# Relu squared in place, one sum per block on GpSimd from block 4 on, and a new order

## The chip, the cores and the metric

The kernel runs on one core of a Trainium2 chip. The metric is the time of one execution in microseconds (us) of device time. Five engines take part, each with its own instruction queue worked off in order: PE (TensorE, matmuls and weight loads), DVE (VectorE), ACT (ScalarE), POOL (GpSimd) and SP (SyncE, which only issues DMAs here). POOL issues DMAs too.

## The reference

Eight batches of eight heads of sparse attention (half of the heads with a local mask of 32, half with a strided one), followed by a feed-forward layer with a squared relu:

```python
B, H, S, D = 8, 8, 576, 64
scores = np.where(masks, q @ k.T / sqrt(D), -1e9)
attn = softmax(scores)
x = (attn @ v).transpose(0, 2, 1, 3).reshape(4608, 512)
h = x @ w_in                      # 512 -> 2048
r = np.maximum(h, 0.0)
out = (s * (r * r) + b) @ w_out   # 2048 -> 512, s and b are single numbers
```

## The kernel before

All matmuls are in 16-bit floats. The 4608 tokens are cut into nine blocks T = 0 to 8 of 512 tokens. The attention of the eight batches (b = 0 to 7, two pairs of local heads and two of strided heads each) makes the rows of x, which the blocks consume. For a block, the first product (`ff1`) makes h in 16 tiles of 128 rows by 512 tokens in PSUM, relu brings each tile to SBUF, and a square of two tiles at a time makes g, the tile `gT` with 16 x 512 columns. There are two `gT` buffers. Relu writes a small buffer `u` (pool `up`, three of 128 x 2 x 512), and the square reads `u` twice and writes `gT`:

```python
nc.scalar.activation(out=u, in_=gts["h", T, ft], func=AF.Relu)
nc.vector.tensor_tensor(out=g, in0=u, in1=u, op=ALU.mult)   # or Square on ACT
```

The second product is done for blocks 2 to 8 by a scheme with seven products P1 to P7 instead of eight (`ff2_seven`). It needs four sums of quarters of `gT`, made in two halves h = 0, 1 of 128 x 1024 elements each (`sums_post`): S3 (a difference, into a tile `S` of its own, of which there is one), then S1, S2 and S4, which all build on S3. S3 of block T can be made only when P7 of block T-1 has read the tile `S`. P7 reads S3, P5 reads S1, P6 reads S2, P3 reads S4. Between the products DVE evicts partial results (`Va`, `Ua`, `Vb`, and `o`, which goes to DRAM), and several products wait for such an eviction before they add to the same PSUM bank: P3 waits for the `o` made from P5 and `Vb`. `Ub` is `Ua` plus a row of constants.

For blocks 7 and 8 the first product is done by a seven-product scheme too (`ff1_seven`), with sums of the weights and of x made on DVE (lines 1099 and 1116), and with additions on DVE in place of some of the relus (line 1161).

Attention steps that matter below: the exponentials come from ACT into `p_loc` or `p_str`, DVE multiplies these by the mask (line 682), then PE multiplies them with v (line 717), and DVE divides by the row sums (lines 734 and 744).

The order of every queue is fixed when the program is made. A planner (`Plan`) walks through a model of the engines: PE steps are taken in an order set by due times, and other work is posted with its needs and its cost on each engine that could do it, and taken in the order of the time at which it became ready plus an offset from a table (`ORDER`, four tables for four stretches of the plan, about 55 numbers each). Nothing is reordered at run time: an engine whose next instruction waits makes everything behind it wait.

POOL issues the loads of q, k and v (`fetch_qk`, `fetch_v`). Ahead of the loads of a batch stand two tiny copies to `gate` (line 1356), which make the queue wait until the transposes of an earlier batch have read their source.

Of the kernel before, what the change touches and what calls it, by code (L numbers as in the profile page):

```python
# [139 lines left out]
class Step:  # L140
    def __init__(self, fn, ns, needs=(), group=None, keys=(), posts=(), after=None):
# [5 lines left out]
ORDER = [  # L147
# [39 lines left out]
]  # L187
# [34 lines left out]
def lay_out(ctx, tc, nc, q, k, v, moe_w_in, moe_w_out, moe_s, moe_b, out, order, q_shape, out_shape,  # L222
# [7 lines left out]
    PS = 512  # L230
# [32 lines left out]
    recp = ctx.enter_context(tc.tile_pool(name="recp", bufs=4))  # L263
    up = ctx.enter_context(tc.tile_pool(name="up", bufs=3))
    gp = ctx.enter_context(tc.tile_pool(name="gp", bufs=2))
# [553 lines left out]
    FIRST7 = NBLK - 2  # L819
    SUM_P = None  # L820
    H = NFT // 2

# [13 lines left out]
    def sums_post(T):  # L836

        at2, at4 = ("S2", "S4") if roomy(T) else ((0, 0), (0, 1))
        for h in range(2):
# [18 lines left out]
            free = [("P7", T - 1)] if T > SEVEN else []  # L858
            plan.post(gl + free, ns, make("S", (0, 0), (1, 0), ALU.subtract), [("S", T, 3, h)])
            plan.post(gh + [("S", T, 3, h)], ns, make((1, 0), (1, 0), (1, 1), ALU.add),  # L860
# [145 lines left out]
    def ff1(T, ft, ct, group, cts=(0, 1, 2, 3), early=False):  # L1006
# [23 lines left out]
        if ct == cts[-1]:  # L1030
            key = ("h", T, ft)
            s.keys = [key] + ([("F1", T)] if ft == NFT - 1 else [])

            at = ff_order(T).index(ft)
            pair = tuple(ff_order(T)[at // 2 * 2:at // 2 * 2 + 2])

            def rl(eng):
                if at % 2 == 0:
                    gts["u", T, pair] = up.tile([128, 2, PS], FP16, tag="u", name="u")
                u = gts["u", T, pair][:, at % 2]  # L1040
                if eng == "A":
                    nc.scalar.activation(out=u, in_=gts["h", T, ft], func=AF.Relu)  # L1042
                else:
                    nc.vector.tensor_relu(out=u, in_=gts["h", T, ft])

            def sq(eng):
                u = gts["u", T, pair]
                g = gts[T][:, pair[0]:pair[0] + 2, :]
                if eng == "A":
                    nc.scalar.activation(out=g, in_=u, func=AF.Square)  # L1050
                else:
                    nc.vector.tensor_tensor(out=g, in0=u, in1=u, op=ALU.mult)  # L1052

            first = at // 2 * 2
            free = ([("g", T, ff_order(T)[first - 6])] if first >= 6 else
                    [("g", T - 1, ff_order(T - 1)[first - 6])] if T else [])
            s.posts = [([key] + free, {"A": 600, **({"V": 690} if T == 0 else {})}, rl, [("u", T, ft), group])]
            if at % 2:
                s.posts.append(([("u", T, x) for x in pair],
                                {"V": 700, **({"A": 1055} if T >= SQ_ACT else {})}, sq,  # L1060
                                [("g", T, x) for x in pair]))
# [58 lines left out]
    def ff1_seven():  # L1120
# [3 lines left out]
        for at, (T, u) in enumerate(units):  # L1124
# [27 lines left out]

            def u_at(row, j, st=st, ft=ft):
                if ("u", row) not in st:
                    st["u", row] = (xnp if row else up).tile(
                        [128, 2, PS], FP16, tag="xs" if row else "u", name="u")
                return st["u", row][:, :, 256 * j:256 * j + 256]

# [15 lines left out]

            def square(row, st=st, T=T, ft=ft):
                def g(eng):
                    if T not in gts:
                        gts[T] = gp.tile([128, NFT, PS], FP16, tag="gT", name="gT")
                    x = st["u", row]
                    g_ = gts[T][:, ft + 8 * row:ft + 8 * row + 2, :]  # L1180
                    if eng == "A":
                        nc.scalar.activation(out=g_, in_=x, func=AF.Square)
                    else:
                        nc.vector.tensor_tensor(out=g_, in0=x, in1=x, op=ALU.mult)
                return g

            def key(x, id_=id_):
                return (x,) + id_

            def was(x, old=old):  # L1190
                return [(x,) + old] if old else []

            far = ff_order(T - 1)[8 + 4 * u:12 + 4 * u] if u < 2 else [
                x + y for x in (ft - 4, ft + 4) for y in (0, 1)]
            free = [("g", T - 1 if u < 2 else T, x) for x in far]
            COPY = {"A": 600.0, "V": 690.0}
# [11 lines left out]
            def wn(n, ft=ft):  # L1208
# [17 lines left out]
                         [key("c21"), Dd]),  # L1226
                        ([key("c21"), key("c22"), ("F2", T - 2)], SQR, square(1),
                         [("g", T, ft + 8), ("g", T, ft + 9)])]),
                "P3": ("A", A, False, s_of(4), x_of(1, 1), xn(1, 1), wn(4) + [key("fe")],
                       [([key("p3")] + free, COPY, relu, [key("c12"), A]),  # L1230
                        ([key("c11"), key("c12"), ("F2", T - 2)], SQR, square(0),
                         [("g", T, ft), ("g", T, ft + 1)])]),
# [405 lines left out]
```

## Time and profile before

| what | value |
|---|---|
| runs | 297.03, 297.75 and 298.77 us, median 297.75 |
| profiled execution, first to last instruction | 295.5 us (the page gives no other time of it) |
| PE busy | 289.5 us, 98% |
| DVE busy | 236.8 us, 80%, 498 instructions |
| ACT busy | 194.6 us, 66%, 334 instructions |
| POOL busy | 92.8 us, 31%, 140 instructions |
| granted TensorE clock | 1.000 |

The table is from the page of the one profiled execution. An instruction counts as busy while it runs or is pipelined; a busy DVE or ACT can still have been waiting for a resource inside an instruction. Times in the views are in us from the start of the span.

### The profile page before, as it was taken

The numbers are of one execution on the slowest core, as the hardware profiler recorded it, in microseconds if no ns is written. First come the engines' busy times: TensorE is split into PE (matmuls) and PEld (weight loads), VectorE is DVE, ScalarE is ACT, GpSimd is POOL, SyncE is SP. The second block draws the span as 40 slices with busy tenths as digits, with TensorE's granted clock in tenths as the row PEclk, the third lists the DMA queues.
The fourth block names the chain that finished last, engine by engine and source line by source line (L and its number), as shares of the span: only waits on it lengthen the run. The fifth ranks groups of instructions, "written<-read, shape, count | busy, mean of one in ns | idle before, by whom it ended". The sixth has DMA issues, their size and how long they took to land.

```text
span 295.5 us, 7106 instructions
## 1 busy us (share of the span) xinstructions
PE 289.5 (98%) x2803; PEld 219.3 (74%) x2803; DVE 236.8 (80%) x498; ACT 194.6 (66%) x334; POOL 92.8 (31%) x140
## 2 busy tenths in 40 slices
PE   7899999999999999999999999999999999999995
PEld 3775655665565567989867785779888999999984
DVE  5765977888976789768986888688899689888874
ACT  3667855897967797947873777478966564576500
POOL 8872623610961396008820195200002000000000
PEclk9999999999999999999999999999999999999999
DMA  8999999999999699979999999998430300210314
GB/s 131 180 206 203 213 184 174 208 189 128 140 160 145 98 91 161 160 138 146 162 149 147 169 168 130 134 137 213 44 104 13 109 35 2 71 38 0 109 39 143
DMA packets 106152, 38.19 MB, mean 129 GB/s; under 512 B 85414, under 2 KB 103974, under 8 KB 106118
## 3 DMA queue, kind: packets, MB, share of 16 engines
q0 software_dynamic: 60848, 18.23, 64.2%
q1 hardware_dynamic: 45270, 19.51, 36.1%
q8 instruction: 22, 0.36, 0.5%
q14 instruction: 12, 0.10, 0.1%
HBM read 36.99 MB, written 10.62 MB: 161 GB/s over the span
## 4 chain that ended last, share of the span: by engine, by line
PE 95%; POOL 3%; DVE 1%; issue 1%; ACT 0%; POOLq 0%
PE ps_f L1016 32%; PE ps_f L984 25%; PE ps_f L1271 8%; PE ps_s L656 5%; PE ps_f L1241 3%; PE ps_a L717 3%; PE ps_t L1241 2%; PE ps_s L984 2%; PE ps_a L1241 2%; PE ps_s L1241 2%; PE ps_t L717 1%; PE ps_t L984 1%; PE ps_s L1271 1%; PE ps_f L717 1%; PE ps_t L535 1%; PE ps_f L535 1%
## 5 line engine op out<-in xcount | busy, mean ns | idle before, releaser
L1016 PE MATMUL ps_f<-xT,w_in_sb 128*128 128x512 f16 (+4 forms) x568 | 115.3, 331 | 0.0
L1042 ACT ACTIVATE u<-ps_f 128x512 f16<-128x512 f32 x107 | 62.8, 595 | 34.5 <-PE ps_f L1016 32.4
L1016 PEld LDWEIGHTS <-w_in_sb 128*128 128x128 f16 x576 | 57.1, 114 | 23.1
L984 PEld LDWEIGHTS <-gT 128*128 128x128 f16 x608 | 58.3, 98 | 8.6
L984 PE MATMUL ps_f<-w_out_sb,gT 128*128 128x256 f16 x376 | 53.4, 273 | 0.0
L1271 PE MATMUL ps_f<-w_out_sb,gT 128*128 128x512 f16 x112 | 31.9, 379 | 0.0
L674 ACT ACTIVATE p_str<-ps_s 72x432 f16<-72x432 f32 (+1 forms) x45 | 21.1, 488 | 10.1 <-PE ps_s L656 9.5
L1052 DVE TENSOR_TENSOR gT<-u 128x1024 f16<-128x1024 f16 x32 | 21.8, 682 | 5.2 <-ACT u L1042 4.8
L1050 ACT ACTIVATE gT<-u 128x1024 f16<-128x1024 f16 x24 | 25.4, 1058 | 0.7
L984 PE MATMUL ps_f<-w_mix,gT 128*128 128x256 f16 x176 | 24.9, 273 | 0.0
L674 ACT ACTIVATE p_loc<-ps_s 128x384 f16<-128x384 f32 x46 | 20.7, 489 | 5.5 <-PE ps_s L656 5.1
L744 DVE TENSOR_TENSOR x_nat<-ps_a,rec 72x384 f16<-72x384 f32 (+2 forms) x45 | 23.5, 523 | 0.7
L852 DVE TENSOR_TENSOR gT<-gT 128x1024 f16<-128x1024 f16 x34 | 22.4, 683 | 0.3 <-ACT gT L1050 0.3
L415 POOL DMA_DIRECT2D v_loc<-in_v_dram x24 | 17.8, 767 | 10.1 <-DMA w_out_sb<-in_moe_w_out_dram 4.2
L984 PEld LDWEIGHTS <-S 128*128 128x128 f16 x176 | 17.1, 98 | 2.7
L717 PEld LDWEIGHTS <-p_str 72*128 72x128 f16 x256 | 13.6, 98 | 5.8 <-ACT p_str L674 0.7
L420 POOL DMA_DIRECT2D v_str<-in_v_dram x16 | 13.0, 817 | 12.8 <-PE ps_f L1016 3.7
L1271 PEld LDWEIGHTS <-gT 128*128 128x128 f16 x128 | 11.4, 98 | 6.9 <-issue 0.2
L1356 POOL COPY gate<-kT 1x1 f16<-1x1 f16 x6 | 2.2, 371 | 45.0 <-DMA kT<-ks 45.0
L984 PE MATMUL ps_f<-w_mix,S 128*128 128x256 f16 x112 | 15.0, 273 | 0.0
L734 DVE RECIPROCAL rec<-ps_a 72x6 f32<-72x6 f32 (+2 forms) x45 | 8.3, 184 | 8.4 <-PE ps_a L717 8.0
L717 PEld LDWEIGHTS <-p_loc 128*128 128x128 f16 x192 | 11.2, 98 | 5.0 <-ACT kTs L437 0.8
(235 smaller groups left out, 543.1 us busy)
## 6 DMA issues: line engine op xcount, KB each, us to landing
out_dram<-o SPq DMA_DIRECT2D x34, 256.0 KB
w_in_sb<-in_moe_w_in_dram POOLq DMA_DIRECT2D x4, 512.0 KB, 9.9
w_out_sb<-in_moe_w_out_dram POOLq DMA_DIRECT2D x4, 512.0 KB, 10.7
qs<-in_q_dram POOLq DMA_DIRECT2D x6, 288.0 KB, 8.1
ks<-in_k_dram POOLq DMA_DIRECT2D x6, 288.0 KB, 9.9
v_loc<-in_v_dram POOLq DMA_DIRECT2D x24, 72.0 KB, 9.8
ql<-in_q_dram POOLq DMA_DIRECT2D x4, 288.0 KB, 9.9
kl<-in_k_dram POOLq DMA_DIRECT2D x16, 72.0 KB, 3.7
```

The source lines that it names most:

```text
L415: nc.gpsimd.dma_start(out=vl[LPAD:128, h, :, 0:D], in_=v_band(b, h))
L674: nc.scalar.activation(out=st["pw", g][0:nk, 0:2 * n * nq], in_=st["s", g][0:nk, 0:2 * n * nq], func=AF.Exp, scale=scale)
L717: nc.tensor.matmul(out=st["pa", g][:, n % 6, :], lhsT=st["pw", gp_][0:nk, i * nq:i * nq + WIDE], rhs=vt[0:nk, 2 * mm + e, j, :])
L744: nc.vector.tensor_tensor(out=x_at(0, cnt), in0=st["pa", g][0:nq, 0:cnt, 0:D], in1=st["rec", g][0:nq, 0:cnt].to_broadcast([nq, cnt, D]), o ...
L852: {"V": nc.vector, "P": nc.gpsimd}[eng].tensor_tensor(out=at(out), in0=at(x), in1=at(y), op=op)
L984: nc.tensor.matmul(out=gts[name, T, t][:, 0] if halves else gts[name, T][:, t], lhsT=lhs(k, t), rhs=rhs(k), start=fresh and k == 0 and (ha ...
L1016: nc.tensor.matmul(out=gts["h", T, ft][:, lo:hi], lhsT=w_in_sb[ft // 4][:, ct].rearrange("p (x l) -> p l x", l=4)[:, ft % 4], rhs=xT[ct][: ...
L1042: nc.scalar.activation(out=u, in_=gts["h", T, ft], func=AF.Relu)
L1050: nc.scalar.activation(out=g, in_=u, func=AF.Square)
L1052: nc.vector.tensor_tensor(out=g, in0=u, in1=u, op=ALU.mult)
L1241: nc.tensor.matmul(out=st[bk][:, 256 * t:256 * t + 256], lhsT=lhs(t, c), rhs=rhs(c), start=fresh and t == c == 0, stop=t == c == 1, skip_g ...
L1271: nc.tensor.matmul(out=gts[id_], lhsT=gts[T][:, ft, ts * 128:(ts + 1) * 128], rhs=w_out_sb[:, ft, cols], start=(ft == 0), stop=(ft == NFT ...
```

## The change

Three things are changed. Relu writes straight into `gT` and the square is done there in place, on the same elements; the buffers `u` go, and with them the waits for a free one. S3 of blocks 4 to 8 is made by POOL and not by DVE, with a planned cost of 3500 ns a half. And the four tables of offsets are new, so that the planner puts much of the work in another order.

```diff
-    up = ctx.enter_context(tc.tile_pool(name="up", bufs=3))
...
+    POOL_SUM = 4
...
             free = [("P7", T - 1)] if T > SEVEN else []
-            plan.post(gl + free, ns, make("S", (0, 0), (1, 0), ALU.subtract), [("S", T, 3, h)])
+            plan.post(gl + free, {"P": 3500.0} if T >= POOL_SUM else ns,
+                      make("S", (0, 0), (1, 0), ALU.subtract), [("S", T, 3, h)])
...
             def rl(eng):
-                if at % 2 == 0:
-                    gts["u", T, pair] = up.tile([128, 2, PS], FP16, tag="u", name="u")
-                u = gts["u", T, pair][:, at % 2]
+                u = gts[T][:, ft]
...
             def sq(eng):
-                u = gts["u", T, pair]
                 g = gts[T][:, pair[0]:pair[0] + 2, :]
                 if eng == "A":
-                    nc.scalar.activation(out=g, in_=u, func=AF.Square)
+                    nc.scalar.activation(out=g, in_=g, func=AF.Square)
                 else:
-                    nc.vector.tensor_tensor(out=g, in0=u, in1=u, op=ALU.mult)
+                    nc.vector.tensor_tensor(out=g, in0=g, in1=g, op=ALU.mult)
...
-            s.posts = [([key] + free, {"A": 600, **({"V": 690} if T == 0 else {})}, rl, [("u", T, ft), group])]
+            s.posts = [([key], {"A": 600, **({"V": 690} if T == 0 else {})}, rl, [("u", T, ft), group])]
...
-            free = [("g", T - 1 if u < 2 else T, x) for x in far]
+            free = [("F2", T - 2)]
...
 ORDER = [
-    {"g": 0.0, "S": -2500.0, "in": 500.0, "w_mix": 2500.0, "wc": 0.0, "ev": 2500.0, "c21": -200.0,
+    {"g": -400.0, "S": -200.0, "in": 500.0, "w_mix": 1500.0, "wc": 0.0, "ev": -400.0,
...
```

PE gets the same instructions as before, matmul for matmul, and the first 528 of its 2801 matmuls stand in the same order. Of the squares, 27 now stand on ACT where 36 stood, and 45 on DVE where 36 stood. One `Ub` goes from POOL to DVE.

On POOL, before, near the end of its queue, where the loads for batch 7 stand (`gate` is the copy that waits for a transpose):

```order
70 L1356 COPY gate<-kT_2571 1x1 x2
71 L387 DMA ql<-in_q_dram 96x6x64 x4
72 L387 DMA kl<-in_k_dram 96x6x64 x4
73 L405 DMA qs<-in_q_dram 72x4x512
74 L405 DMA ks_120<-in_k_dram 72x4x512
75 L415 DMA v_loc_102<-in_v_dram 96x6x64 x4
76 L420 DMA v_str_104<-in_v_dram 72x8x64 x4
77 L926 ISA
78 L926 TENSOR_TENSOR Ub<-Ua,bcs 128x512
```

And the same place of the same queue now:

```order
70 L853 ISA
71 L853 TENSOR_TENSOR S<-gT 128x1024 x2
72 L1346 COPY gate<-kT_2527 1x1 x2
73 L387 DMA ql<-in_q_dram 96x6x64 x4
74 L387 DMA kl<-in_k_dram 96x6x64 x4
75 L405 DMA qs<-in_q_dram 72x4x512
76 L405 DMA ks_117<-in_k_dram 72x4x512
77 L415 DMA v_loc_99<-in_v_dram 96x6x64 x4
78 L420 DMA v_str_101<-in_v_dram 72x8x64 x4
79 L853 TENSOR_TENSOR S<-gT 128x1024 x8
```

The two halves of S3 of block 4 stand ahead of the loads for batch 7, and the eight of blocks 5 to 8 behind them; the `Ub` is gone.

On DVE, before, where S3 of block 4 is made, from the `Vb` of block 3 on (`o` from `Vb` is the eviction that P3 waits for; the mask is that of batch 6):

```order
267 L903 SCALAR_TENSOR_TENSOR Vb<-ps_f_162,sb_all,Ub 128x512
268 L852 TENSOR_TENSOR S<-gT 128x1024 x2
269 L852 TENSOR_TENSOR gT<-gT 128x4x256
270 L915 SCALAR_TENSOR_TENSOR o<-ps_f_163,sb_all,Vb 128x512
271 L852 TENSOR_TENSOR gT<-gT 128x4x256
272 L682 TENSOR_TENSOR p_loc_115<-p_loc_115,masks 128x1152
```

The same place on DVE now:

```order
266 L905 SCALAR_TENSOR_TENSOR Vb<-ps_f_159,sb_all,Ub 128x512
267 L1051 TENSOR_TENSOR gT<-gT 128x1024
268 L917 SCALAR_TENSOR_TENSOR o<-ps_f_160,sb_all,Vb 128x512
269 L853 TENSOR_TENSOR gT<-gT 128x4x256
270 L682 TENSOR_TENSOR p_loc_112<-p_loc_112,masks 128x1152
```

The two halves of S3 are gone, a square (line 1051) stands there, and of the two halves of S1 (line 853, `gT<-gT`) only the first is still ahead of the mask.

On DVE, before, one block later, from the `Vb` of block 4 to the mask of batch 7:

```order
310 L903 SCALAR_TENSOR_TENSOR Vb<-ps_f_162,sb_all,Ub 128x512
311 L437 COPY qD_loc_108<-qTl 64x6x96 x2
312 L852 TENSOR_TENSOR S<-gT 128x1024 x2
313 L852 TENSOR_TENSOR gT<-gT 128x4x256
314 L915 SCALAR_TENSOR_TENSOR o<-ps_f_163,sb_all,Vb 128x512
315 L437 COPY v_loc_102<-v_loc_102 32x2x5x64
316 L852 TENSOR_TENSOR gT<-gT 128x4x256
317 L915 SCALAR_TENSOR_TENSOR o<-ps_f_162,sb_all,Ua 128x512
318 L682 TENSOR_TENSOR p_loc_115<-p_loc_115,masks 128x1152
```

And now:

```order
309 L905 SCALAR_TENSOR_TENSOR Vb<-ps_f_159,sb_all,Ub 128x512
310 L437 COPY qD_loc_105<-qTl 64x6x96 x2
311 L1051 TENSOR_TENSOR gT<-gT 128x1024
312 L917 SCALAR_TENSOR_TENSOR o<-ps_f_160,sb_all,Vb 128x512
313 L437 COPY v_loc_99<-v_loc_99 32x2x5x64
314 L853 TENSOR_TENSOR gT<-gT 128x4x256
315 L917 SCALAR_TENSOR_TENSOR o<-ps_f_159,sb_all,Ua 128x512
316 L682 TENSOR_TENSOR p_loc_112<-p_loc_112,masks 128x1152
```

Here too a square stands where the two halves of S3 stood, and the second half of S1 has gone behind the mask.

More of the change, by code (lines that the diff above doesn't have):

```diff
@@ L1046, in sq @@
             def sq(eng):
-                u = gts["u", T, pair]
                 g = gts[T][:, pair[0]:pair[0] + 2, :]
                 if eng == "A":
-                    nc.scalar.activation(out=g, in_=u, func=AF.Square)
+                    nc.scalar.activation(out=g, in_=g, func=AF.Square)
                 else:
-                    nc.vector.tensor_tensor(out=g, in0=u, in1=u, op=ALU.mult)
-            first = at // 2 * 2
-            free = ([("g", T, ff_order(T)[first - 6])] if first >= 6 else
-                    [("g", T - 1, ff_order(T - 1)[first - 6])] if T else [])
-            s.posts = [([key] + free, {"A": 600, **({"V": 690} if T == 0 else {})}, rl, [("u", T, ft), group])]
+                    nc.vector.tensor_tensor(out=g, in0=g, in1=g, op=ALU.mult)
+            s.posts = [([key], {"A": 600, **({"V": 690} if T == 0 else {})}, rl, [("u", T, ft), group])]
             if at % 2:
@@ L1151, in keep, with u_at @@
                 return g
[L1153 to L1157, printed above, removed]
+            def u_at(row, j, T=T, ft=ft):
+                if T not in gts:
+                    gts[T] = gp.tile([128, NFT, PS], FP16, tag="gT", name="gT")
+                return gts[T][:, ft + 8 * row:ft + 8 * row + 2, 256 * j:256 * j + 256]
             def add(row, j, of, name, st=st, u_at=u_at):
@@ L1173, in relu, with square @@
                         "p (t x) -> p t x", t=2))
-            def square(row, st=st, T=T, ft=ft):
+            def square(row, T=T, ft=ft):
                 def g(eng):
-                    if T not in gts:
-                        gts[T] = gp.tile([128, NFT, PS], FP16, tag="gT", name="gT")
-                    x = st["u", row]
                     g_ = gts[T][:, ft + 8 * row:ft + 8 * row + 2, :]
                     if eng == "A":
-                        nc.scalar.activation(out=g_, in_=x, func=AF.Square)
+                        nc.scalar.activation(out=g_, in_=g_, func=AF.Square)
                     else:
-                        nc.vector.tensor_tensor(out=g_, in0=x, in1=x, op=ALU.mult)
+                        nc.vector.tensor_tensor(out=g_, in0=g_, in1=g_, op=ALU.mult)
                 return g
@@ L1191, in was @@
                 return [(x,) + old] if old else []
-            far = ff_order(T - 1)[8 + 4 * u:12 + 4 * u] if u < 2 else [
-                x + y for x in (ft - 4, ft + 4) for y in (0, 1)]
-            free = [("g", T - 1 if u < 2 else T, x) for x in far]
+            free = [("F2", T - 2)]
             COPY = {"A": 600.0, "V": 690.0}
@@ L1226, in ff1_seven @@
                          [key("c21"), Dd]),
-                        ([key("c21"), key("c22"), ("F2", T - 2)], SQR, square(1),
+                        ([key("c21"), key("c22")], SQR, square(1),
                          [("g", T, ft + 8), ("g", T, ft + 9)])]),
@@ L1230, in ff1_seven @@
                        [([key("p3")] + free, COPY, relu, [key("c12"), A]),
-                        ([key("c11"), key("c12"), ("F2", T - 2)], SQR, square(0),
+                        ([key("c11"), key("c12")], SQR, square(0),
                          [("g", T, ft), ("g", T, ft + 1)])]),
```

77 rows, old and new, of the table ORDER are left out of this document.

## The prediction

> **What bounds the kernel.** I read the windows first, then the chain and PE's waits. Columns of the windows: length, then busy time and instructions of PE, PEld, DVE, ACT and POOL, granted clock, DMA.
>
> ```profile
> 0.00:22.00 22.00, 19.10 (x262) 13.27 (x263) 15.15 (x51) 11.80 (x28) 18.16 (x33) 1.00 1.15 172
> 22.00:215.00 193.00, 193.00 (x1836) 135.13 (x1835) 155.27 (x334) 143.50 (x253) 73.03 (x106) 1.00 1.34 154
> 215.00:250.00 35.00, 35.00 (x325) 31.70 (x322) 31.07 (x60) 21.48 (x31) 1.65 (x1) 1.00 0.17 52
> 250.00:292.40 42.40, 42.36 (x389) 39.17 (x386) 34.79 (x54) 17.85 (x24) 0.00 (x0) 1.00 0.17 58
> 292.40:295.50 3.10, 0.00 (x0) 0.00 (x0) 0.48 (x1) 0.00 (x0) 0.00 (x0) 1.00 0.48 165
> ```
>
> ```profile
> PE 95%; POOL 3%; DVE 1%; issue 1%; ACT 0%; POOLq 0%
> ```
>
> ```profile
> PE ps_t L527 <- DMA ql<-in_q_dram: 0.9, 1, 0.9
> ...
> PE ps_f L717 <- DVE v_loc L437: 0.7, 1, 0.7
> PE ps_f L717 <- POOL v_loc L437: 0.4, 1, 0.4
> ```
>
> From 22.0 to 292.4 us PE misses 0.04 us, at full clock; its waits lie in the first 22 us (2.9 us idle), and the last 3.1 us are the last eviction and store. The changed program has the same matmuls, and the first 528 in the same order, so the head stays. An engine relieved beside a PE that never waits gives nothing back: the most to win is a fraction of the 0.04 us. The forecast is therefore a question of new PE waits, and every such wait adds its whole length, since no gap lies behind it to take it up.
>
> **The change part by part.** *Buffers and squares.*
>
> ```profile
> L1042 ACT ACTIVATE u<-ps_f 128x512 f16<-128x512 f32 x107 | 62.8, 595 | 34.5 <-PE ps_f L1016 32.4
> L1050 ACT ACTIVATE gT<-u 128x1024 f16<-128x1024 f16 x24 | 25.4, 1058 | 0.7
> L852 DVE TENSOR_TENSOR gT<-gT 128x1024 f16<-128x1024 f16 x34 | 22.4, 683 | 0.3 <-ACT gT L1050 0.3
> ```
>
> Of the relus' 34.5 us idle, 32.4 were for PE, so the buffers cost next to nothing and dropping them brings nothing. DVE sums that write over their own input take 683 ns, like others, so a square in place costs the same; on ACT that isn't shown, and I take 1058 ns, with ACT's 34% of idle time as cover. Nine squares fewer are 9 x 1.058 = 9.5 us less ACT; on DVE they are +9 x 0.68 = 6.1, the ten S3 halves -10 x 0.68 = -6.8, one `Ub` +0.69: nothing in sum. The relu of the last two blocks needs its `gT` free earlier than the square did; that isn't shown, and goes into the 0 to 0.5 us of blocks 6 to 8 below.
>
> *S3 on POOL: how long a half takes.* One POOL sum of two tensors is in the trace, and what DVE did beside it:
>
> ```profile
> 221.54 1.65 POOL L926 TENSOR_TENSOR Ub<-Ua,bcs 128x512 f32<-128x512 f32 x1 [33.35 <-DVE Ua L903]
> ```
>
> ```profile
> 221.38 0.67 DVE L1099 TENSOR_TENSOR ks<-ks,w_in_sb 128x1024 f16<-128x1024 f16 x1
> 222.60 1.14 DVE L852 TENSOR_TENSOR S<-gT 128x1024 f16<-128x1024 f16 x1 [0.55 <-PE ps_f L984]
> ```
>
> The DVE sum at 222.60 took 1.14 us where its kind takes 0.683. POOL ended at 221.54 + 1.65 = 223.19, and 223.19 - 222.60 = 0.59 of waiting plus 0.55 of work is 1.14: DVE stood until POOL had finished. The other way round, the DVE sum that had begun at 221.38 ended at 222.05 undisturbed, and from there POOL needed 1.14 us. So while one reads two tensors of SBUF the other waits, and 1.14 us for 512 elements makes 2 x 1.14 = 2.28 us for the 1024 of a half. Bounds: 2 x 1.65 = 3.30 if POOL had not waited, and below, by POOL's copies of one tensor (611 ns for 512 elements), 1.22. I take 2.28, as nearest in kind.
>
> ```profile
> L437 POOL COPY v_str<-vs 72x512 f16<-72x512 f16 x4 | 2.3, 611 | 2.1 <-DMA vs<-in_v_dram 2.1
> ```
>
> The Trainium skill ("GPSIMD Engine Reference", Performance versus the Vector engine) gives 4497 ns for a sum of 2048 elements; an estimate from it is 2.25 us a half, against the 3.30 of my upper bound, and the sum by it would be 300.3 us.
>
> The same lock shows with copies from SBUF to SBUF, and that POOL can get in between two adjacent DVE instructions:
>
> ```profile
> 79.42 0.97 DVE L437 COPY qD_str<-qT 64x576 f16<-64x576 f16 x2
> 79.53 1.40 POOL L437 COPY qD_str<-qT 64x576 f16<-64x576 f16 x2
> ```
>
> ```profile
> L437 DVE COPY qD_loc<-qTl 64x576 f16<-64x576 f16 x10 | 3.0, 302 | 0.1
> ```
>
> Two such copies otherwise take some 0.6 us; here 0.97, since the second stood until POOL's first was done.
>
> *S3 of block 4.* Rows of before at that place, DVE and then PE:
>
> ```profile
> 165.29 0.75 DVE L903 SCALAR_TENSOR_TENSOR Vb<-ps_f,sb_all,Ub 128x512 f32<-128x512 f32 x1
> 165.96 1.28 DVE L852 TENSOR_TENSOR S<-gT 128x1024 f16<-128x1024 f16 x2
> 167.16 0.69 DVE L852 TENSOR_TENSOR gT<-gT 128x1024 f16<-128x1024 f16 x1
> 167.90 0.75 DVE L915 SCALAR_TENSOR_TENSOR o<-ps_f,sb_all,Vb 128x512 f32<-128x512 f32 x1
> 168.57 0.68 DVE L852 TENSOR_TENSOR gT<-gT 128x1024 f16<-128x1024 f16 x1
> 169.79 0.76 DVE L682 TENSOR_TENSOR p_loc<-p_loc,masks 128x1152 f16<-128x1152 f16 x1 [0.54 <-ACT p_loc L674]
> ```
>
> ```profile
> 164.55 0.71 PE L984 MATMUL ps_f<-w_mix,S 128*128 128x256 f16 x5
> 170.88 0.35 PE L717 MATMUL ps_a<-v_loc,p_loc 128*128 128x65 f16 x6
> ```
>
> P7 ends at 165.26 and both halves of S3 can start. POOL: 165.3 to 167.6. DVE evicts `Vb` beside it (one of its tensors is in PSUM; such evictions keep their 0.75 us, and I count them as free of the lock). The square that now follows has its relu at about 167.0 and stands until 167.6, so 168.15. POOL's second half: 168.15 to 170.43. `o` to 168.8; the first half of S1 stands until 170.43, so 170.98; the mask ends at about 171.7, against 170.55 before. The product with v began at 170.88, 0.33 us behind the mask: PE now waits **0.85 us**. With 3.30 a half it is 2.9, with 1.22 nothing.
>
> *S3 of block 5.*
>
> ```profile
> 195.10 0.75 DVE L903 SCALAR_TENSOR_TENSOR Vb<-ps_f,sb_all,Ub 128x512 f32<-128x512 f32 x1 [0.85 <-PE ps_f L984]
> 195.77 0.61 DVE L437 COPY qD_loc<-qTl 64x576 f16<-64x576 f16 x2
> ...
> 199.95 0.74 DVE L915 SCALAR_TENSOR_TENSOR o<-ps_f,sb_all,Ua 128x512 f32<-128x512 f32 x1
> 200.91 0.76 DVE L682 TENSOR_TENSOR p_loc<-p_loc,masks 128x1152 f16<-128x1152 f16 x1 [0.22 <-ACT p_loc L674]
> ```
>
> ```profile
> 194.36 0.71 PE L984 MATMUL ps_f<-w_mix,S 128*128 128x256 f16 x5
> 202.10 0.35 PE L717 MATMUL ps_a<-v_loc,p_loc 128*128 128x65 f16 x6
> ```
>
> POOL: 195.1 to 197.4. The first copy stands until then, the second behind POOL's other half, 197.6 to 199.9. From 200.1 DVE has, start to start, the square 0.60, `o` 0.66, a copy 0.33, S1 0.60, `o` 0.66: the mask starts at 202.95 and ends at 203.7. The product with v, at 202.10 before, waits **1.6 us**. With 3.30 a half 3.6; with 1.22 the mask would be done by 201.6, in time.
>
> *S3 of blocks 6 to 8.* At block 6 DVE was ahead of PE (it stood 0.55 us for PE before the row at 222.60), so its two-tensor sums are through before POOL starts; behind, POOL and DVE alternate without a mask. In blocks 7 and 8 the halves come singly, each at most some 2 us, ahead of evictions with about a microsecond to spare. I take 0.2 us for the three, from 0 to 0.5.
>
> *POOL's queue.* The loads of batch 7 now stand behind two halves of S3:
>
> ```profile
> 167.32 0.57 POOL L1356 COPY gate<-kT 1x1 f16<-1x1 f16 x1 [15.65 <-DMA kT<-ks]
> 169.59 0.75 POOL L387 DMA_DIRECT2D ql<-in_q_dram  x1 [0.30 <-issue]
> ```
>
> ```profile
> L607 SPq DMA_TRANSPOSE qTl<-ql x6: 1212/1391/2904, 119.7 to 182.1; - x6
> ```
>
> `gate` goes from 167.32 to about 170.4, so the loads from 169.59 to some 171.4, and with them the transposes on SP that end with that of 182.1. Their result is copied at 195.77: over 12 us of cover for 1.8. Nothing, and it would cost only what exceeds those 12 us.
>
> *Sum.* 0.85 + 1.6 + 0.2 = 2.65 us. The profiled execution has a span of 295.5 us; the median of the runs, 297.75, is 2.25 more and I let that stand: **300.4 us**. Bounds: all terms nothing 297.75; at 3.30 a half 2.9 + 3.6 + 0.5 = 7.0, so 304.75.
>
> **The rivals.** *Not slower: POOL is the one that stands.* Where DVE asks first, POOL waits, as from 221.54 to 222.05. A half has 3.5 us in the plan, so 2.28 with two waits of 0.6 still fits, DVE keeps its times, and it is 297.75. It decides where DVE's next two-tensor instruction starts before P7 has ended. Against it: in blocks 4 and 5 DVE has the eviction `Vb` first, which waits for the same P7. The Trainium skill ("SBUF — State Buffer", Who interferes with whom) says that issue order decides who blocks; by that rule the time is 297.75 where DVE is first and 300.4 where POOL is; the trace agrees with both rows above. *The lock is harmless: POOL is fast.* Near 1.22 us a half the masks come in time: 297.75 too; for it only the copies speak. *POOL is slow.* Sums in 16 bits and with a stride are not in the trace; from 3.5 us a half on S1 is late in blocks 4 and 5 and DVE's queue stands for it: 304.75 or more. *The new order alone costs:* masks precede their products by 0.33 us, so a landing or an exponential late by 1 us anywhere in the new order costs its excess; some three such give 299.
>
> **How the numbers follow.** Forecast (two waits of 0.5 to 3 us) 0.5; no visible wait, by one of the first two rivals, 0.3; slow POOL 0.1; the order alone 0.1. The runs of before spread by 1.7 us, so 0.5%, 1.5 us, is about what can be told from no change. Slower by more: 0.5 x 0.85 + 0.1 + 0.1 x 0.5, and something of the rest, 0.6; faster 0.07, from the spread alone, since no mechanism here wins; within, 0.33. The range takes in no change less some spread and most of the slow POOL: 297.2 to 304.
>
> **What would show it.** Right: ten POOL sums of about 2.3 us, in pairs at some 165 and 195 us; DVE squares, S1 or copies beside them stretched from 0.68 to up to 3 us; PE waits at the product with v behind masks of batches 6 and 7 of 0.5 to 2 us each; the same head; ACT busy down by some 9 us. Wrong: PE without waits behind 22 us, or PE waits at other places, and POOL's spans stretched instead of DVE's.

## The result, and the profile after

The changed kernel took 300.04 us (median of four runs, 299.98 to 300.13), the kernel before 297.61 us (four runs, 297.03 to 298.77): a ratio of 1.0081, 95% interval 1.0058 to 1.0103. Predicted were 300.4 us, in a range from 297.2 to 304. The profiled span grew from 295.5 to 298.2 us, at full clock.

The windows of the changed kernel (columns as before) and PE's waits:

```profile
22.00:215.00 193.00, 190.84 (x1801) 132.71 (x1800) 155.98 (x323) 140.35 (x250) 82.55 (x110) 1.00 1.37 153
215.00:250.00 35.00, 35.00 (x337) 31.49 (x335) 29.27 (x63) 21.43 (x32) 4.22 (x2) 1.00 0.18 56
```

```profile
PE ps_f L986 <- DVE o L917: 1.3, 1, 1.3
PE ps_a L717 <- DVE p_loc L682: 0.8, 2, 0.7
```

PE, which missed nothing there before, now misses 193.00 - 190.84 = 2.16 us between 22 and 215 us, in three waits, and nothing from 215 to 250 us. PE's share of the chain of work that ended last falls from 95% to 92%. The waits in PE's own rows (line 986 is `ff2_seven`, line 717 the product with v, line 656 the scores):

```profile
170.43 0.27 PE L986 MATMUL ps_f<-w_mix,gT 128*128 128x256 f16 x1
171.36 0.36 PE L717 MATMUL ps_a<-v_loc,p_loc 128*128 128x65 f16 x6 [0.66 <-DVE p_loc L682]
...
199.65 1.04 PE L986 MATMUL ps_f<-w_mix,gT 128*128 128x256 f16 x8
202.01 0.49 PE L986 MATMUL ps_f<-w_out_sb,gT 128*128 128x256 f16 x3 [1.32 <-DVE o L917]
...
203.98 0.27 PE L986 MATMUL ps_f<-w_out_sb,gT 128*128 128x256 f16 x1
204.42 0.27 PE L717 MATMUL ps_a<-v_loc,p_loc 128*128 128x65 f16 x3 [0.17 <-DVE p_loc L682]
```

A matmul of 256 columns is followed by the next 0.11 us later where nothing waits (eight in 0.87 us). Measured from start to start, PE therefore lost 0.83 us at 170.4 (block 4), 1.49 us at 200.5 and 0.33 us at 204.1 (block 5): 2.65 us of the span's 2.7. What DVE and POOL did there, block 4 first and then block 5:

```profile
165.39 0.75 DVE L905 SCALAR_TENSOR_TENSOR Vb<-ps_f,sb_all,Ub 128x512 f32<-128x512 f32 x1 [0.24 <-PE ps_f L986]
167.10 1.01 DVE L1051 TENSOR_TENSOR gT<-gT 128x1024 f16<-128x1024 f16 x1 [0.96 <-ACT gT L1042]
168.03 0.74 DVE L917 SCALAR_TENSOR_TENSOR o<-ps_f,sb_all,Vb 128x512 f32<-128x512 f32 x1
168.69 1.95 DVE L853 TENSOR_TENSOR gT<-gT 128x1024 f16<-128x1024 f16 x1
170.56 0.74 DVE L682 TENSOR_TENSOR p_loc<-p_loc,masks 128x1152 f16<-128x1152 f16 x1
...
196.71 3.87 DVE L437 COPY qD_loc<-qTl 64x576 f16<-64x576 f16 x2
200.60 0.69 DVE L1051 TENSOR_TENSOR gT<-gT 128x1024 f16<-128x1024 f16 x1
201.22 0.74 DVE L917 SCALAR_TENSOR_TENSOR o<-ps_f,sb_all,Vb 128x512 f32<-128x512 f32 x1
```

```profile
165.44 4.65 POOL L853 TENSOR_TENSOR S<-gT 128x1024 f16<-128x1024 f16 x2 [12.85 <-PE ps_f L986]
...
196.14 4.26 POOL L853 TENSOR_TENSOR S<-gT 128x1024 f16<-128x1024 f16 x2 [7.35 <-issue]
```

The evictions `Vb` and `o` run beside POOL at their 0.75 us. The square (1.01 us), S1 (1.95 us) and above all the two copies (3.87 us, where such a pair takes some 0.6) end only when a POOL half has ended. The copies depend on nothing that POOL makes.

### The profile page after: what moved, and what is told of

The parts are those of the page before. It is cut to its first block, busy times and chain, and to the rows that moved or that the text cites. A ratio compares the mean times of both kernels' runs of the same rounds, so it can differ in the third digit from the quotient of the medians.

```text
span 298.2 us, 7095 instructions
## 1 busy us (share of the span) xinstructions
PE 290.8 (98%) x2803; PEld 219.3 (74%) x2803; DVE 238.5 (80%) x491; ACT 189.7 (64%) x332; POOL 113.8 (38%) x149
## 4 chain that ended last, share of the span: by engine, by line
PE 92%; POOL 3%; DVE 3%; issue 1%; ACT 0%; POOLq 0%
PE ps_f L1018 32%; PE ps_f L986 24%; PE ps_f L1261 8%; PE ps_s L656 4%; PE ps_f L1231 3%; PE ps_a L717 3%; PE ps_t L1231 2%; PE ps_s L1231 2%; PE ps_s L986 2%; PE ps_a L1231 1%; PE ps_t L717 1%; PE ps_t L986 1%; PE ps_s L1261 1%; PE ps_f L717 1%; PE ps_t L535 1%
## 5 line engine op out<-in xcount | busy, mean ns | idle before, releaser
L1042 ACT ACTIVATE gT<-ps_f 128x512 f16<-128x512 f32 x107 | 62.8, 595 | 33.7 <-PE ps_f L1018 32.6
L853 POOL TENSOR_TENSOR S<-gT 128x1024 f16<-128x1024 f16 x10 | 22.1, 2219 | 89.4 <-PE ps_f L986 59.3
L1051 DVE TENSOR_TENSOR gT<-gT 128x1024 f16<-128x1024 f16 x37 | 25.7, 695 | 8.3 <-ACT gT L1042 7.8
L853 DVE TENSOR_TENSOR gT<-gT 128x1024 f16<-128x1024 f16 x34 | 23.7, 719 | 0.3
L1049 ACT ACTIVATE gT<-gT 128x1024 f16<-128x1024 f16 x19 | 20.1, 1058 | 0.5
```

The costliest lines, as they stand in the source:

```text
L853: {"V": nc.vector, "P": nc.gpsimd}[eng].tensor_tensor(out=at(out), in0=at(x), in1=at(y), op=op)
L1049: nc.scalar.activation(out=g, in_=g, func=AF.Square)
L1051: nc.vector.tensor_tensor(out=g, in0=g, in1=g, op=ALU.mult)
```

## The experiments

Theory: DVE's instructions with two SBUF tensors, and its copies from SBUF to SBUF, stand while POOL reads SBUF (the lock), and PE waits for what is queued behind them. Rivals: the new order costs it; the squares in place cost it; POOL sums cost by their number; DVE only waits for S3's result. Spans are those of the profiled runs.

| kernel | S3 on POOL | median us | ratio to before, 95% | span us |
|---|---|---|---|---|
| changed | blocks 4 to 8 | 300.04 | 1.0058 to 1.0103 | 298.2 |
| same order, all on DVE | none | 297.23 | 0.9960 to 1.0015 | 295.3 |
| same order | 4 | 298.00 | 0.9986 to 1.0019 | 296.2 |
| same order | 5 | 299.08 | 1.0026 to 1.0059 | 297.2 |
| same order | 6 to 8 | 297.34 | 0.9966 to 1.0002 | 295.4 |
| planned anew | 6 to 8 | 299.11 | 1.0037 to 1.0072 | 297.1 |
| old table, buffers `u` | 4 to 8 | 306.17 | 1.0255 to 1.0319 | 305.4 |
| old table, in place | none | 297.33 | 0.9975 to 1.0008 | 296.2 |
| extra POOL sums | 4 to 8 | 311.06 | 1.0408 to 1.0467 | 308.9 |
| POOL copies | 4 to 8 | 297.59 | 0.9995 to 1.0038 | 295.7 |
| POOL memsets | 4 to 8 | 297.54 | 0.9987 to 1.0018 | 295.3 |
| two buffers for S | 4 to 8 | 302.49 | 1.0145 to 1.0197 | 301.2 |

The kernel before itself scatters from 297.03 to 301.23 us (and took 610.71 us once), its medians of the sets from 297.47 to 297.87. Differences under 1 us are therefore read from the spans and PE's rows.

**The same order without POOL.** PE's order is the same, instruction by instruction; DVE has ten instructions more.

```diff
-                    {"V": nc.vector, "P": nc.gpsimd}[eng].tensor_tensor(
+                    {"V": nc.vector, "P": nc.vector}[eng].tensor_tensor(
```

> The changed kernel, with every instruction in its place, but the ten S3 halves issued on DVE at the point of the order where POOL's were issued. If the cost is that DVE's two-tensor instructions stand while POOL makes S3 (lock theory): no S3 on POOL, so no wait at blocks 4 and 5 although DVE has ten instructions of 0.68 us more; PE idle behind 22 us under 0.5 us, time within 0.5 us of the kernel before (297.6). If the new order of the program costs it (order rival): the 2.4 us stay, 300.0. If squares in place cost it: 300.0 as well.

Measured: 297.23 us, span 295.3, and PE is busy for 193.00 of the 193.00 us from 22 to 215 us. The new order, and the squares in place with it, cost nothing; the 2.65 us hang on POOL making S3.

**In place alone.** The kernel before with its own table and with the squares in place, so without the buffers `u`.

```diff
-                    gts["u", T, pair] = up.tile([128, 2, PS], FP16, tag="u", name="u")
+                u = gts[T][:, ft]
...
-                    nc.vector.tensor_tensor(out=g, in0=u, in1=u, op=ALU.mult)
+                    nc.vector.tensor_tensor(out=g, in0=g, in1=g, op=ALU.mult)
```

> The kernel before with its own table of priorities, relu and square in place without buffers between, S3 on DVE throughout. Lock theory and order rival: PE without waits behind 22 us, 297.6 within 0.5 us, though ACT has some 5 to 9 us less work. In-place rival (a square over its own input is slower, or gT is wanted earlier): up to 300.

Measured: 297.33 us, not to be told from the kernel before. PE misses 0.23 us between 22 and 215 us in the profiled execution, where none was expected; that is small beside the 2.16 us of the changed kernel. In the changed kernel an ACT square in place takes what one out of `u` took:

```profile
L1049 ACT ACTIVATE gT<-gT 128x1024 f16<-128x1024 f16 x19 | 20.1, 1058 | 0.5
```

**Block by block, in one order.** Only the engine of S3 differs.

```diff
-                    {"V": nc.vector, "P": nc.gpsimd}[eng].tensor_tensor(
+                    {"V": nc.vector, "P": nc.gpsimd if T in (4,) else nc.vector}[eng].tensor_tensor(
```

with `(5,)` and `(6, 7, 8)` in the other two.

> The changed kernel in its own order, with the two S3 halves of block 4 on POOL and those of blocks 5 to 8 issued on DVE at the same points. Lock theory: the wait of block 4 alone, at the product with v of batch 6, 0.83 us; time 0.8 us over the kernel before (298.3), and no wait at block 5. Rival (POOL sums cost by their number, wherever they stand): 2/10 of 2.4 us, 0.5 us over.

> The changed kernel in its own order, with the two S3 halves of block 5 alone on POOL, the others on DVE at the same points. Lock theory: the two waits of block 5, 1.49 us at P3 for the eviction o and 0.34 us at the product with v of batch 7, 1.8 us over the kernel before (299.4). Rival (number alone): 0.5 us over (298.1).

> The changed kernel in its own order, with the six S3 halves of blocks 6 to 8 on POOL and those of blocks 4 and 5 on DVE. Lock theory, with the place of DVE's instructions deciding: in this order no DVE instruction with two SBUF tensors stands behind Vb in block 6, so no wait, 297.6 within 0.5 us, though the kernel with S3 on POOL from block 6 on in a planned order of its own took 299.1. Rival (the six halves cost by themselves, or the 2.65 us of waits ahead had hidden them): 299.1.

Measured: PE's rows lose 0.83 us in the first (all of it at the product with v of batch 6), 1.44 + 0.34 us in the second, nothing in the third. Against the span of 295.3 us without POOL that is +0.9, +1.9 and +0.1, together 2.9, and the changed kernel has +2.9: the places add up, and the number of sums does not matter. Against the noisy median of before, the first cannot be told from no change; there the span and the row carry it.

**Blocks 6 to 8 in an order planned anew.**

```diff
-    POOL_SUM = 4
+    POOL_SUM = 6
```

> The changed kernel with S3 on POOL from block 6 on instead of from block 4 (six halves instead of ten). Lock theory: the waits of blocks 4 and 5 go, POOL's halves in blocks 6 to 8 cost 0 to 0.5 us, time 297.6 to 298.1. Order rival: 300. If it is the number of POOL sums that counts, wherever they stand: 6/10 of 2.4 us, 299.0.

A miss: 299.11 us, where the same six halves in the changed kernel's order cost nothing. The planner, run with S3 on DVE in blocks 4 and 5, had put one sum of weights behind `Vb`:

```profile
224.12 0.75 DVE L905 SCALAR_TENSOR_TENSOR Vb<-ps_f,sb_all,Ub 128x512 f32<-128x512 f32 x1 [0.91 <-PE ps_f L986]
224.79 2.11 DVE L1095 TENSOR_TENSOR v_str<-w_in_sb,ks 128x1024 f16<-128x1024 f16 x1
```

```profile
PE ps_s L1231 <- DVE qD_loc L1112: 0.9, 1, 0.9
```

It stood 1.4 us, S1 after it 0.5 us (1.15 us long), and PE waited for the sums of x behind both. From start to start PE lost 1.3 us there and another 0.4 us at 239.5, where it waited for a copy of ACT; why that copy was late was not tried. In the changed kernel's order DVE has only the evictions `Vb` and `o` there, and S1 comes at 231.11, when POOL has 0.2 us left. What decides is which instruction of DVE comes next when POOL starts.

**Only S3 on POOL, in the kernel before.**

```diff
-            plan.post(gl + free, ns, make("S", (0, 0), (1, 0), ALU.subtract), [("S", T, 3, h)])
+            plan.post(gl + free, {"P": 3500.0} if T >= 4 else ns,
+                      make("S", (0, 0), (1, 0), ALU.subtract), [("S", T, 3, h)])
```

> The kernel before with its own table of priorities and its buffers, and only S3 of blocks 4 to 8 on POOL. Lock theory: POOL halves of 2.1 to 2.3 us in pairs at some 165 and 195 us, DVE sums, squares or copies beside them stretched, PE waits of 0.5 to 3 us in all in blocks 4 and 5, time 298.5 to 301. Order rival and in-place rival: no extra wait, 297.6.

The direction is as expected, the size isn't: 306.17 us, where 298.5 to 301 was expected. Blocks 4 and 5 lose 2.8 us, much as in the changed kernel; block 6 is new. DVE, then POOL, at that place:

```profile
225.38 0.68 DVE L1100 TENSOR_TENSOR ks<-ks,w_in_sb 128x1024 f16<-128x1024 f16 x1
225.98 0.69 DVE L1100 TENSOR_TENSOR v_str<-w_in_sb,ks 128x1024 f16<-128x1024 f16 x1
...
228.39 0.28 DVE L1117 TENSOR_TENSOR p_loc<-xT,p_loc 128x256 f16<-128x256 f16 x1
228.59 0.74 DVE L904 SCALAR_TENSOR_TENSOR Vb<-ps_f,sb_all,Ub 128x512 f32<-128x512 f32 x1
230.70 2.60 DVE L852 TENSOR_TENSOR gT<-gT 128x1024 f16<-128x1024 f16 x1 [1.36 <-POOL S L852]
```

```profile
225.43 7.32 POOL L852 TENSOR_TENSOR S<-gT 128x1024 f16<-128x1024 f16 x2 [25.29 <-PE ps_f L985]
```

Here DVE had a row of eight two-tensor instructions, from 225.38 to some 228.6, and POOL was the one that stood: its first half released DVE at 230.70, and 230.70 - 2.13 = 228.57 is where it can have begun to work. DVE then waited 1.36 us for the result, and S1 stood for POOL's second half. PE waited 3.42 us for the sums of x that follow, and then ran at half clock:

```profile
233.00:236.70 3.70, 0.28 (x4) 0.12 (x2) 3.70 (x10) 0.00 (x0) 0.00 (x0) 0.82 0.20 71
236.70:242.20 5.50, 5.50 (x27) 3.79 (x27) 1.15 (x5) 0.58 (x1) 0.00 (x0) 0.50 0.15 51
242.20:250.00 7.80, 7.80 (x73) 7.40 (x72) 5.89 (x10) 4.49 (x7) 0.00 (x0) 1.00 0.10 34
```

5.5 us at 0.50 cost another 2.75 us. In block 8 a square stood for a half of S3 (2.39 us long, at 288.63), and PE lost 0.8 us behind it at 292.8. With the 3.42 us, which are 3.58 from start to start, these make 9.9 us, as much as the span grew (305.4 - 295.5).

**POOL sums that nobody waits for.**

```diff
+                    if out == "S" and T >= POOL_SUM and fs.start:
+                        for k in (0, 4):
+                            nc.gpsimd.tensor_tensor(out=spare[:, k:k + 4], in0=gts["S", T][:, k:k + 4],
+                                                    in1=gts["S", T][:, k:k + 4], op=ALU.add)
```

> The changed kernel in its own order, but behind each block's second S3 half POOL makes two more sums of the same size, S plus S into a tile that nobody reads; no engine waits for them by a semaphore. Lock theory: DVE's next two-tensor instructions (mask and copies in block 4, square, copies and S1 in block 5) stand for them as well, 2 to 4 us of PE waits more in each of blocks 4 and 5, 304 to 308. Rival (DVE only waits for S3's result, nothing is locked): 300.0, as without them.

Measured: 311.06 us. In block 4 POOL makes the extra sums from 170.05 on, and DVE's rows are:

```profile
170.56 2.44 DVE L682 TENSOR_TENSOR p_loc<-p_loc,masks 128x1152 f16<-128x1152 f16 x1
172.93 2.32 DVE L437 COPY qD_str<-qT 64x576 f16<-64x576 f16 x2
```

```profile
170.05 4.70 POOL L858 TENSOR_TENSOR spare<-S 128x1024 f16<-128x1024 f16 x2
```

No semaphore ties these instructions to POOL's, and still the mask takes 2.44 us where it took 0.74. That DVE only waits for S3 is out. The time lies above the expected range because I had reckoned only with blocks 4 and 5: PE also lost 1.4, 2.3 and 1.4 us in blocks 6, 7 and 8, and after a wait of 2.90 us in block 5 its clock was 0.60 for 4.3 us.

**A shorter POOL instruction, and one that only writes.** In place of the sum, which both kernels leave out:

```diff
+                        nc.gpsimd.tensor_copy(out=at(out), in_=at(x))
```

and in the other kernel:

```diff
+                        for _ in range(2):
+                            nc.gpsimd.memset(at(out), 0.25)
```

> The changed kernel in its own order, but each of the ten S3 halves on POOL is a copy of one tensor (S becomes the first term; the subtraction is left out), which should take 1.22 us by POOL's copies of 512 elements in 611 ns. Lock theory: DVE stands half as long; o and the masks then come in time or nearly, PE waits of 0 to 0.5 us in all, 297.5 to 298. Rival (POOL's place in the chain from S3 to S1 costs, or POOL's instruction as such, whatever its length): above 299.

> The changed kernel in its own order, but each of the ten S3 halves on POOL is two memsets of S, 1024 elements each (S becomes a constant; the subtraction is left out), which only write. Lock theory as the traces have it so far (it is the reading of SBUF tensors that excludes): squares and sums on DVE beside them keep 0.69 us, no wait in block 4; for the copies of block 5 nothing is shown yet, 0 to 1.5 us; time 297.3 to 299. Rival (any POOL instruction on SBUF holds DVE's two-tensor instructions): DVE rows beside the memsets are stretched by what is left of the memset, as for the sum. The Trainium skill (SBUF — State Buffer, Who interferes with whom) says that a DVE instruction with two SBUF inputs contends with a POOL instruction that reads SBUF, and not with one that only writes it.

Measured: a copy takes 1.04 us undisturbed, and PE waits nowhere behind the head: 297.59 us. With the memsets 297.54 us, though POOL is busy there for 3.86 and 4.07 us, about as long as with the sums. DVE in blocks 4 and 5, and POOL:

```profile
166.90 0.69 DVE L1055 TENSOR_TENSOR gT<-gT 128x1024 f16<-128x1024 f16 x1 [0.96 <-ACT gT L1046]
...
168.47 0.68 DVE L857 TENSOR_TENSOR gT<-gT 128x1024 f16<-128x1024 f16 x1
...
195.67 1.58 DVE L437 COPY qD_loc<-qTl 64x576 f16<-64x576 f16 x2
```

```profile
165.22 3.86 POOL L855 MEMSET S<- 128x1024 f16 x4 [13.20 <-PE ps_f L990]
...
195.09 4.07 POOL L855 MEMSET S<- 128x1024 f16 x4 [8.23 <-PE ps_f L990]
```

The square and S1 (line 857) beside a memset keep their 0.69 and 0.68 us, so neither the length of POOL's work nor DVE's need of its result is what stretches such instructions beside the sums. The copies still stand, the pair for about as long as one memset of 0.95 us. So it is POOL's reading that holds up a two-tensor instruction, while a copy is held up by a POOL instruction that only writes as well. The Trainium skill (SBUF — State Buffer, Who interferes with whom) states the first case, and of copies that they can contend with GpSimd in a mode that uses both ports of VectorE; the rows agree with the first, and whether these copies ran in that mode no run shows.

**Two buffers for S.**

```diff
-            free = [("P7", T - 1)] if T > SEVEN else []
+            free = [("P7", T - 2)] if T > SEVEN + 1 else []
```

with a pool of two tiles for `S`.

> The changed kernel with two buffers for S, so that S3 of a block need not wait for P7 of the block before; the planner then places everything anew. If the cost is only that POOL's halves fall where DVE has copies, squares and sums due within 2 us: the halves start earlier, where DVE's results have more time, and the waits of blocks 4 and 5 shrink, 297.5 to 299. If POOL's halves fall on other urgent two-tensor instructions of DVE: 299 to 301, with PE waits at other places. Order rival: nothing can be told in numbers, since the order is another.

Measured: 302.49 us, the second of the expected outcomes in kind, but above its 299 to 301. Block 4 is cured. In block 5 S3 now lies in POOL's queue behind a load that POOL could issue only at 187.46, and DVE stood for S3; later `Ub` falls beside POOL's other half. In block 6 a sum (at 222.71) stands for POOL's second half:

```profile
190.46 0.69 DVE L854 TENSOR_TENSOR gT<-gT 128x1024 f16<-128x1024 f16 x1 [5.24 <-POOL S L854]
...
194.91 2.06 DVE L929 TENSOR_TENSOR Ub<-Ua,bcs 128x512 f32<-128x512 f32 x1
...
222.71 2.62 DVE L854 TENSOR_TENSOR gT<-gT 128x1024 f16<-128x1024 f16 x1
```

PE lost 1.5 us in block 5 and 3.1 us in block 6, 2.05 of these in one wait for the sums of x at 231.7, at the end of a DVE queue that had no pause since that sum. Starting earlier moved the collisions; since the order is another too, how much of the span's 5.7 us is due to the order stays open. No kernel here beats the kernel before beyond the scatter; the nearest are the changed order with S3 on DVE throughout and with it on POOL in blocks 6 to 8 alone (297.23 and 297.34 us).

## Why the prediction was right

*PE is the bound and new waits add in full:* right. The three waits sum to 2.65 us, the span grew by 2.7 and the median by 2.4. The head is the same: 262 matmuls have been started by 22.0 us in both.

*Buffers and squares cost nothing:* right by the runs without POOL. The nine ACT squares went (36 to 27), but ACT's busy time fell by 4.9 us and not by some 9: other work of 4.6 us came to ACT, which I had left out, without effect on the time.

*2.28 us a half:* nearly. Undisturbed halves take 2.12 to 2.13 us (the pair at 196.14 took 4.26); the ten have a mean of 2.22 with what they waited. The estimate worked out from the Trainium skill (GPSIMD Engine Reference, Performance versus the Vector engine), 2.25 us, lies 6% above the 2.13 measured.

*Block 4, 0.85 us:* right in mechanism and place, and in size partly by luck. The square ended at 168.11 (worked out: 168.15), S1 at 170.64 (170.98), the mask at 171.31 (171.7), and the wait was 0.83 us at the product named. The mask came 0.4 us earlier than worked out, with POOL's shorter halves; but PE was also ready for the product earlier, at 170.43 + 0.11 = 170.54 and not at 170.88. The prediction took 170.88 from the order before, and in the new order four matmuls fewer (0.44 us) stand between P7 and this product. The two errors cancel. The block alone on POOL gave the same 0.83.

*Block 5, 1.6 us:* the cause is right, the place only in part. The copies ended at 200.58, `o` at 201.96. The step "the product with v, at 202.10 before, waits 1.6 us" looked only at the end of DVE's late chain; its earlier consumer is P3, which needs that `o` and was due at 200.52. PE waited 1.49 us there, and with PE itself late only 0.33 us remained at the product with v: 1.82 in all, 0.2 more than predicted. The missed wait is not where the 0.2 comes from: without it PE would have been ready for the product with v at 204.09 - 1.49 = 202.60, and would have waited the same 1.82 us until 204.42. Here too four matmuls fewer stand ahead of that product than in the order before.

*Blocks 6 to 8, 0.2 us:* nothing was lost, and the reason given for block 6 (DVE's two-tensor sums are through before POOL starts) is what the run with the newly planned order shows by its opposite. The sum came out exact by luck: 0.2 too much here met 0.2 too little in block 5.

*POOL's queue:* right. The loads of batch 7 were issued from 171.29 (worked out: 171.4), and no wait follows from it.

*The rivals.* That POOL is the one that stands is a real case, seen in block 6 of the old table, but not where `Vb` goes ahead, and it was no cover: DVE then waited for POOL. That a fast POOL is harmless is shown by the copies of 1.04 us; the sum isn't that fast, and slow POOL falls by the same 2.13 us. The new order alone cost nothing.

## What to carry to other kernels

Work moved to GpSimd can cost VectorE time: look at which VectorE instruction is queued at the moment when GpSimd starts, and if GpSimd reads SBUF and VectorE reads two tensors there, price it as standing for the rest of the GpSimd instruction; do the same for a copy from SBUF to SBUF. Evictions that read one of their tensors from PSUM kept their time here. Then follow the delayed queue to each of its consumers on the bounding engine, the first included, and read from the new order, not from the old one, when that engine will need their results. Where that engine never waits, an engine relieved beside it brings nothing, so there is no gain to set against such a risk.

## What was not expected of the hardware

The lock does not change hands at every boundary. POOL got in between two copies of DVE (3.87 us for the pair), but with DVE's two-tensor instructions in a row it stood for 3.1 us (225.43 to 228.57) and was not let in between them. Those instructions overlap (0.69 us long, 0.60 us apart), and the copies don't; whether that is the reason was not tried.

Longer waits of PE can carry a second price: the clock fell to 0.50 for 5.5 us after a wait of 3.42 us, and to 0.60 over the 4.3 us after one of 2.90 us, while one of 2.4 us left it at 1.00. The Trainium skill (TensorE: Matmul & The Clock Gate, Part 1: The HAM clock gate) gives half rate after about 3.4 us of idling; the first of these agrees, the second came after less. This second price is not fixed: six executions of the kernel before with S3 on POOL had spans from 302.5 us, at a mean clock of 1.000, to 305.6 us, at 0.989. After the waits of the changed kernel, at most 1.5 us, the clock stayed at 1.00.
